# Other half-steps for the side work of six batches, ScalarE in pieces of 512 columns, wider block turns

## The chip, the cores and the metric

The kernel runs on one core of a Trainium2 chip. The metric is device time in microseconds of one execution; the kernel before has a median of 707.55 us in three runs. Times below are microseconds unless marked ns. PE is TensorE's matmul queue, PEld its weight loads, DVE VectorE, ACT ScalarE, POOL GpSimd, SP the engine that issues most DMAs (SPq in the rows).

## What is computed

An attention through 32 memories per head, followed by a two-layer network with a squared ReLU. Cut to what matters:

```python
a = softmax(phi, over the sequence)               # B 8, H 8, S 576, M 32
k_m, v_m = a^T k, a^T v                           # per head 32 x 64
attn = softmax(q k_m^T / 8, over the memories)    # S x 32 per head
x = (attn v_m) laid out as tokens x 512           # 4608 x 512
h = max(x w_in, 0)                                # w_in 512 x 2048
out = (h * h) w_out                               # w_out 2048 x 512
```

The kernel never forms x. Per batch it folds v_m into w_in, which gives `u` (four chunks n = 0 to 3 of 512 columns of w_in, as a high and a low part), and the first layer multiplies `u` with the attention weights `a` (also high and low). Both are split so that three fast products stand for one exact product.

## The kernel before, in words

**Two parts ahead of the second layer.** Batches 0 and 1 run through `runs`, a list of steps that interleaves both layers (up to about 213 us). Batches 2 to 7 run in the loop at the end of the function: per batch 16 steps (f = 0 to 15, 128 rows of the hidden layer each), and then one second layer for all six (from 427 us). This document is about the loop.

**A step** of the loop: `first_layer(b, f, ...)` puts 12 matmuls of 128x288 (two halves of the tokens) into a PSUM tile `hh`, of which there are two; ScalarE then takes ReLU of it into half of a tile `o` (`r`); `half(2 * k)` and `half(2 * k + 1)` write out the side work that is due in the two half-steps; `spill()` writes a full `o` (two steps, 576 KB) to the DRAM tensor `r_f`. There are two `o` tiles, so the third pair of steps waits until the first one's spill has landed, and the matmuls of step f+2 wait for the ReLU of step f.

**Side work** of batch b is the table `later`: for each task the half-steps (of 32 per batch, counted from the batch's first) in which its parts are issued, and the batch it is for, as an offset.

- `task_phi`, `task_kv`, `task_q`: loads, all on SP's queue, which issues in order.
- `task_exp` (`exp_phi_blocks`): the maximum of phi over the sequence on DVE (`phi_mx`, `top`), the subtraction into `e_sb`, then Exp on ACT. It is for the batch after the next.
- `task_mem` (`memories_in_h`): 80 small matmuls of `e_sb` with the loaded k and v, normalised into a tile `st` and turned in 32x32 blocks into `mem`.
- `task_u` (`make_u`): 16 matmuls into the one tile `ps_m`, a copy to `u_hi` on ACT, the rest to `u_lo` on DVE, which frees `ps_m`.
- `task_attend` (`attend`): 8 pairs of score matmuls from `q_sb` (one buffer), then on DVE block turns into `st`, maximum, subtraction, on ACT Exp, on DVE sum, reciprocal, product, block turns into `at`; on ACT the high part `a_hi` (or `o`, `r_room`, which also serve as rooms for it), on POOL the low part.

Engines take their instructions in the order in which the loop writes them, so the table fixes each engine's queue. In it the k-th step of a batch is written out before the side work of half-steps 2k and 2k+1. `STEP` is 32 half-steps, `begin` the first of batch 2 (`FUSED`). A task whose list passes 32 runs into the next batch: `task_u, 1, 2` at 32 to 34 is chunk 2 of the batch that has just begun.

Of the kernel before, what the change touches and what calls it, by code (L numbers as in the profile page):

```python
# [8 lines left out]
F32 = mybir.dt.float32  # L9
# [3 lines left out]
AF = mybir.ActivationFunctionType  # L13
ALU = mybir.AluOpType
# [10 lines left out]
def attn_moe_kernel(ctx: ExitStack, tc: tile.TileContext, qT, kv, phi, w_in, w_out, outT):  # L25
# [20 lines left out]
    D = 64  # L46
    M = 32
# [182 lines left out]
    def exp_phi_blocks(b, e):  # L230

        w = NQ * P
        nb = w // M
        mx = one.tile([P, w], F32, name="phi_mx")
        nc.vector.tensor_tensor(out=mx, in0=e[0], in1=e[1], op=ALU.max)
        for x in e[2:-1]:
            nc.vector.tensor_tensor(out=mx, in0=mx, in1=x, op=ALU.max)  # L237
# [4 lines left out]
        tr = one.tile([P, w], F32, name="at")  # L242
# [12 lines left out]
        for x in e[:-1]:  # L255
            nc.vector.tensor_tensor(out=x, in0=x, in1=mx, op=ALU.subtract)
# [40 lines left out]
    def memories_in_h(b, kvs, mem):  # L297


        assert ("phi", b) in ready  # L300
# [16 lines left out]
        ready.add(("read", b))  # L317
        den = work.tile([P, NQ], F32, name="den")
        kvn = one.tile([P, 2, NQ, 2, D], F32, name="st")
        for qd in range(NQ):  # L320
            nc.vector.tensor_scalar_add(den[:, qd:qd + 1], acc[qd][:, 2 * D:2 * D + 1], EPS)
            nc.vector.reciprocal(den[:, qd:qd + 1], den[:, qd:qd + 1])
            nc.vector.tensor_scalar_mul(
                kvn[:, :, qd],
                acc[qd][:, :2 * D].rearrange("p (x d) -> p x d", x=2)[:, :, None, :].broadcast_to([P, 2, 2, D]),
                den[:, qd:qd + 1],
            )
        yield
# [233 lines left out]
    def make_u(b, n, mem, w, got):  # L562
# [9 lines left out]
        nc.scalar.copy(u_hi[:, :, n0:n1], ps[:, :, :n1 - n0])  # L572
# [407 lines left out]
    for n in kept:  # L980
# [63 lines left out]
        ((87, 88, 88), task_mem, 2),  # L1044
# [17 lines left out]
        ((112, 113, 113), task_u, 2, 2),  # L1062
# [11 lines left out]
    for places, fn, *args in plan:  # L1074
# [9 lines left out]
        ((2, 3, 5), task_mem, 1),  # L1084
        ((3,), task_phi, 2),
        ((4, 6, 8, 10, 12), task_kv, 2, 0),
        ((14, 16, 18, 20, 22), task_kv, 2, 1),
        ((8, 9, 10), task_u, 0, 3),
        ((9, 10, 11, 12, 13, 14, 15), task_attend, 1, 0),
        ((10,), task_q, 1, 1),  # L1090
        ((16, 17, 18), task_u, 1, 0),
        ((18, 19, 20, 21, 22, 23, 24), task_attend, 1, 1),
        ((19,), task_q, 2, 0),
        ((24, 25, 26), task_u, 1, 1),
# [410 lines left out]
```

## Time and profile before

| | |
|---|---|
| median of three runs | 707.55 us (706.66 to 708.33) |
| the profiled execution: its own time, its span | 708.06 us, 706.2 us |
| PE busy | 686.6 us, 97% of the span |
| DVE, ACT, POOL busy | 531.6, 395.8, 59.1 us |
| granted TensorE clock | 0.999 |
| from batch 3's memories (221.48 us) to batch 7's (369.04 us) | four periods of one batch each |
| second layer begins | 427.12 us |

The granted clock is at its upper level (2.4 GHz) throughout. In the rows, a timeline line reads: start, duration, engine, source line, operation, output<-inputs, shape, count, and in brackets the idle time of the engine before it and what ended it. Matmuls of one step stand in six lines of two; the line with `a_hi,u_hi` begins a step.

### The profile page before, as it was taken

The numbers are of one execution on the slowest core, as the hardware profiler recorded it, in microseconds if no ns is written. First come the engines' busy times: TensorE is split into PE (matmuls) and PEld (weight loads), VectorE is DVE, ScalarE is ACT, GpSimd is POOL, SyncE is SP. The second block draws the span as 40 slices with busy tenths as digits, with TensorE's granted clock in tenths as the row PEclk, the third lists the DMA queues.
The fourth block names the chain that finished last, engine by engine and source line by source line (L and its number), as shares of the span: only waits on it lengthen the run. The fifth ranks groups of instructions, "written<-read, shape, count | busy, mean of one in ns | idle before, by whom it ended". The sixth has DMA issues, their size and how long they took to land.

```text
span 706.2 us, 14494 instructions
## 1 busy us (share of the span) xinstructions
PE 686.6 (97%) x5860; PEld 612.8 (87%) x5860; DVE 531.6 (75%) x967; ACT 395.8 (56%) x575; POOL 59.1 (8%) x86
## 2 busy tenths in 40 slices
PE   9899999999999989899989999999999999999997
PEld 4477798988888778787878899999999999999996
DVE  4978797987776686867676403989988979697984
ACT  2648887866553444444444546766655565555551
POOL 1222102102220000000000000000000000000000
PEclk9999999999999999999999999999999999999999
DMA  9992537354794949494954358753364544435331
GB/s 307 391 349 104 199 111 230 103 168 131 203 342 152 322 162 315 158 319 165 316 188 168 146 201 301 262 174 111 90 180 119 151 120 129 140 117 153 90 120 60
DMA packets 94354, 133.58 MB, mean 189 GB/s; under 512 B 5520, under 2 KB 59408, under 8 KB 93648
## 3 DMA queue, kind: packets, MB, share of 16 engines
q1 hardware_dynamic: 91472, 127.62, 56.2%
q10 hardware_dynamic: 2816, 5.05, 1.9%
q8 instruction: 46, 0.75, 0.4%
q14 instruction: 20, 0.16, 0.1%
HBM read 86.51 MB, written 46.14 MB: 188 GB/s over the span
## 4 chain that ended last, share of the span: by engine, by line
PE 76%; DVE 12%; DMA 4%; ACT 4%; issue 2%; SPq 0%; POOL 0%; ACTq 0%; DVEq 0%
PE b L1293 33%; PE hh L1425 11%; PE acc L743 10%; PE h L692 7%; PE b L1276 5%; PE acc L735 3%; PE ps_m L426 3%; PE h L304 2%; DMA r_f<-o 2%; DMA wo<-in_w_in 1%; DVE phi_mx L237 1%; DMA u_hi<-in_kv 1%; DVE at L488 1%; DVE st L485 1%; DVE sm L474 1%
## 5 line engine op out<-in xcount | busy, mean ns | idle before, releaser
L1227 DVE TENSOR_TENSOR x_lo<-y,x_hi 128x1792 fp32r<-128x1792 f32 (+1 forms) x56 | 104.7, 1870 | 49.7 <-ACT x_hi L1223 49.7
L1223 ACT CAST x_hi<-y 128x1792 fp32r<-128x1792 f32 (+1 forms) x56 | 87.9, 1570 | 96.2 <-PE b L1293 52.1
L1293 PE MATMUL b<-x_lo,s_hi 128*128 128x256 f32 x384 | 108.1, 281 | 0.0
L1293 PE MATMUL b<-x_hi,wo 128*128 128x256 f32 x576 | 107.9, 283 | 0.0
L1293 PE MATMUL b<-x_hi,s_hi 128*128 128x256 f32 x384 | 107.9, 281 | 0.0
L1293 PE MATMUL b<-x_hi,s_lo 128*128 128x256 f32 x384 | 107.9, 281 | 0.0
L1456 ACT ACTIVATE o<-hh 128x576 f32<-128x576 f32 x94 | 60.8, 650 | 68.2 <-PE hh L1425 37.7
L1293 PEld LDWEIGHTS b<-x_hi,wo 128*128 128x128 f32 x576 | 89.9, 192 | 0.0
L1293 PE MATMUL b<-x_lo,wo 128*128 128x256 f32 x288 | 81.5, 283 | 0.4 <-DVE x_lo L1227 0.3
L574 DVE TENSOR_TENSOR u_lo<-ps_m,u_hi 128x1024 fp32r<-128x1024 f32 (+1 forms) x33 | 39.3, 1190 | 52.6 <-ACT u_hi L572 52.4
L1216 DVE TENSOR_TENSOR y<-y 128x512 f32<-128x512 f32 x144 | 73.7, 512 | 3.4
L1293 PEld LDWEIGHTS b<-x_hi,s_hi 128*128 128x128 f32 x384 | 73.7, 192 | 0.0
L1293 PEld LDWEIGHTS b<-x_lo,s_hi 128*128 128x128 f32 x384 | 72.1, 188 | 0.0
L1293 PEld LDWEIGHTS b<-x_hi,s_lo 128*128 128x128 f32 x384 | 72.1, 188 | 0.0
L1206 ACT ACTIVATE y<-raw 128x1024 f32<-128x1024 f32 (+1 forms) x56 | 57.4, 1025 | 12.3 <-DMA raw<-r_f 9.8
L1293 PEld LDWEIGHTS b<-x_lo,wo 128*128 128x128 f32 x288 | 55.3, 192 | 0.8 <-DVE x_lo L1227 0.8
L1425 PEld LDWEIGHTS hh<-a_hi,u_hi 128*128 128x128 f32 x188 | 29.3, 188 | 24.8 <-ACT o L1456 14.9
L1425 PE MATMUL hh<-a_hi,u_hi 128*128 128x288 f32 x188 | 44.4, 317 | 3.4 <-ACT o L1456 3.2
L743 PE MATMUL acc<-g_hi,wo 128*128 128x320 f32 (+1 forms) x256 | 43.2, 301 | 0.0
L1425 PE MATMUL hh<-a_hi,u_lo 128*128 128x288 f32 x188 | 40.2, 295 | 0.0
L1425 PE MATMUL hh<-a_lo,u_hi 128*128 128x288 f32 x188 | 40.1, 294 | 0.0
L700 ACT ACTIVATE r_room<-h 128x320 f32<-128x320 f32 (+2 forms) x56 | 24.7, 441 | 27.5 <-PE h L692 26.6
(234 smaller groups left out, 1442.2 us busy)
## 6 DMA issues: line engine op xcount, KB each, us to landing
r_f<-o SPq DMA_DIRECT2D x48, 576.0 KB, 4.4
raw<-r_f SPq DMA_DIRECT2D x48, 512.0 KB, 4.0
wo<-in_w_in SPq DMA_DIRECT2D x16, 512.0 KB, 8.2
wo<-in_w_out SPq DMA_DIRECT2D x16, 512.0 KB, 6.9
kvb<-in_kv SPq DMA_DIRECT2D x28, 256.0 KB, 6.2
q_sb<-in_q SPq DMA_DIRECT2D x24, 288.0 KB, 5.1
out_t<-m SPq DMA_DIRECT2D x24, 256.0 KB, 2.3
e_sb<-in_phi SPq DMA_DIRECT2D x8, 512.0 KB, 4.3
```

Of the source, the lines that this page charges most:

```text
L574: nc.vector.tensor_tensor(out=u_lo[:, :, n0:n1], in0=ps[:, :, :n1 - n0], in1=u_hi[:, :, n0:n1].bitcast(F32), op=ALU.subtract)
L692: nc.tensor.matmul(h[:, at:at + n], u[:, qd, fs], x[:, qd], start=(i == 0), stop=(i == len(todo) - 1))
L700: nc.scalar.activation(r, h[:, :T], AF.Relu)
L743: nc.tensor.matmul(acc[e][:, :T], wo[f][:, w, e * P:(e + 1) * P], x, start=first and x is g_hi and w == 0, stop=last and x is g_lo,)
L1206: nc.scalar.activation(y[i][:, :2 * n], raw.pop(i), AF.Square)
L1216: nc.vector.tensor_tensor(out=out, in0=in0, in1=in1, op=ALU.subtract)
L1223: nc.scalar.copy(x[i][0], y[i])
L1227: nc.vector.tensor_tensor(out=x[i][1], in0=y.pop(i), in1=x[i][0].bitcast(F32), op=ALU.subtract)
L1276: nc.tensor.matmul(acc[e][:, :n], wo[f][:, v, e * P:(e + 1) * P], x[i][u][:, f % 2 * n:(f % 2 + 1) * n], start=f == 0 and j == 0, stop=f = ...
L1293: nc.tensor.matmul(acc[m][:, e * HALF:(e + 1) * HALF], w, x[i][u][:, z * HALF:(z + 1) * HALF], start=p == 0 and e == 0 and j == 0, stop=p ...
L1425: nc.tensor.matmul(banks[t][:, :T], u[:, qd, fs], x[:, qd], start=(i == 0), stop=(i == len(todo) - 1))
L1456: nc.scalar.activation(r.rearrange("p (t x) -> p t x", t=NT), h[:, :, :S // NT], AF.Relu)
```

## The change

It rewrites the table `later` (every task at other half-steps; Exp of phi ends at half-step 26 instead of 31; chunk 2 of `u` is now listed under its own batch, at 0, 1, 3; memories begin at 1 instead of 2; the load of the second half of q goes from 10 to 12, the scores that read it from 18 to 17). For batch 2 alone memories stay later, at 4 to 8, and phi and the k and v loads shift by 3. ScalarE's copy to `u_hi` becomes two of 512 columns, Exp of `e_sb` two of 512 and one of 128. In `memories_in_h` the product with 1/den goes from DVE to ACT (`kvn`, without the second copy that it had), and 8 block turns of 32x(4x32) replace 16 of 32x(2x32). In `exp_phi_blocks` the maximum becomes a tree with a second tile, and four subtractions become one of 1024 columns. From batch 4 on, that second tile is `a_hi1` instead of `at`.

```diff
+        tr = place([P, w], F32, name="a_hi1") if b > FUSED + 1 else one.tile([P, w], F32, name="at")
         nc.vector.tensor_tensor(out=mx, in0=e[0], in1=e[1], op=ALU.max)
-        for x in e[2:-1]:
-            nc.vector.tensor_tensor(out=mx, in0=mx, in1=x, op=ALU.max)
+        nc.vector.tensor_tensor(out=tr, in0=e[2], in1=e[3], op=ALU.max)
+        nc.vector.tensor_tensor(out=mx, in0=mx, in1=tr, op=ALU.max)
...
-        for x in e[:-1]:
-            nc.vector.tensor_tensor(out=x, in0=x, in1=mx, op=ALU.subtract)
+        nc.vector.tensor_tensor(
+            out=full, in0=full, in1=mx[:, None, :].broadcast_to([P, nfull, w]), op=ALU.subtract
+        )
...
-        nc.scalar.activation(e_sb[:, :nfull], e_sb[:, :nfull], AF.Exp)
-        nc.scalar.activation(e[nfull], e[nfull], AF.Exp)
+        for x in (full[:, :2], full[:, 2:], e[nfull]):
+            nc.scalar.activation(x, x, AF.Exp)
...
+        yield
         den = work.tile([P, NQ], F32, name="den")
-        kvn = one.tile([P, 2, NQ, 2, D], F32, name="st")
         for qd in range(NQ):
             nc.vector.tensor_scalar_add(den[:, qd:qd + 1], acc[qd][:, 2 * D:2 * D + 1], EPS)
-            nc.vector.reciprocal(den[:, qd:qd + 1], den[:, qd:qd + 1])
-            nc.vector.tensor_scalar_mul(
...
+        nc.vector.reciprocal(den, den)
+        yield
+        kvn = one.tile([P, 2, NQ, D], F32, name="st")
+        for qd in range(NQ):
+            nc.scalar.activation(
+                kvn[:, :, qd], acc[qd][:, :2 * D].rearrange("p (x d) -> p x d", x=2), AF.Copy,
+                scale=den[:, qd:qd + 1],
             )
...
-                    nc.vector.transpose(
-                        mem[at:at + M, x, j // 2::2], kvn[M * j:M * (j + 1), x, :, 0, M * k:M * (k + 1)]
-                    )
+                nc.vector.transpose(
+                    mem[at:at + M, :, j // 2::2], kvn[M * j:M * (j + 1), :, :, M * k:M * (k + 1)]
+                )
...
-        nc.scalar.copy(u_hi[:, :, n0:n1], ps[:, :, :n1 - n0])
+        for half in range(2) if b >= FUSED else (slice(2),):
+            nc.scalar.copy(u_hi[:, half, n0:n1], ps[:, half, :n1 - n0])
...
     later = [
-        ((2, 3, 5), task_mem, 1),
...
-        ((24, 26, 27, 28, 29, 31), task_exp, 2),
...
+        ((1, 2, 5, 6, 7), task_mem, 1),
...
+        ((12, 13, 16, 17, 21, 26), task_exp, 2),
...
```

**ScalarE, second half of batch 5** (`o` ReLU of a step, L471 and L474 Exp of the scores, L491 and L494 the high part of the weights, L261 to L264 Exp of `e_sb`). Before:

```order
L1456 ACTIVATE o_4314<-hh 128x576
L1456 ACTIVATE o_4381<-hh 128x576
L471 ACTIVATE st<-st 128x576
L1456 ACTIVATE o_4381<-hh 128x576
L1456 ACTIVATE o_4426<-hh 128x576
L491 CAST o_4410<-at 128x576
L572 CAST u_hi_4430<-ps_m 128x1024
L1456 ACTIVATE o_4426<-hh 128x576
L1456 ACTIVATE o_4487<-hh 128x576 x2
L261 ACTIVATE e_sb<-e_sb 128x1024
L262 ACTIVATE e_sb<-e_sb 128x128
L1456 ACTIVATE o_4527<-hh 128x576
```

After:

```order
L1463 ACTIVATE o_4365<-hh 128x576 x2
L474 ACTIVATE st<-st 128x576
L576 CAST u_hi_4386<-ps_m 128x512 x2
L1463 ACTIVATE o_4422<-hh 128x576 x2
L264 ACTIVATE e_sb<-e_sb 128x512 x2
L264 ACTIVATE e_sb<-e_sb 128x128
L494 CAST o_4404<-at 128x576
L1463 ACTIVATE o_4458<-hh 128x576 x2
L1463 ACTIVATE o_4488<-hh 128x576
```

Exp of `e_sb` stood behind the last ReLU of the batch and ahead of the first of the next; now it stands two steps earlier, behind step 13, with the high part of the weights right behind it.

**VectorE, the same stretch** (`phi_mx`, `top`: the maximum of phi; L574 and L578 `u_lo`; L457 to L488, L460 to L491 the softmax of the scores). Before:

```order
L240 TENSOR_TENSOR phi_mx<-phi_mx,e_sb 64x128 x2
L574 TENSOR_TENSOR u_lo_4431<-ps_m,u_hi_4430 128x1024
L243 STREAM_TRANSPOSE at<-phi_mx 128x256
L245 TENSOR_REDUCE top<-at 128x8
L248 TENSOR_TENSOR top<-top 32x8 x3
L250 COPY top<-top 32x8 x3
L252 COPY at<-top 128x256
L253 STREAM_TRANSPOSE phi_mx<-at 128x256
L256 TENSOR_TENSOR e_sb<-e_sb,phi_mx 128x256 x4
L258 TENSOR_TENSOR e_sb<-e_sb,phi_mx 64x128 x2
L574 TENSOR_TENSOR u_lo_4530<-ps_m,u_hi_4529 128x1024
```

After:

```order
L255 STREAM_TRANSPOSE phi_mx<-a_hi_4233 128x256
L578 TENSOR_TENSOR u_lo_4261<-ps_m,u_hi_4260 128x1024
L460 STREAM_TRANSPOSE st<-h 128x288 x2
L466 TENSOR_REDUCE mx<-st 128x18
L472 TENSOR_TENSOR st<-st,mx 128x576
L257 TENSOR_TENSOR e_sb<-e_sb,phi_mx 128x1024
L261 TENSOR_TENSOR e_sb<-e_sb,phi_mx 64x128 x2
L477 TENSOR_REDUCE sm<-st 128x18
L480 TENSOR_SCALAR sm<-sm 128x18
L483 RECIPROCAL sm<-sm 128x18
L488 TENSOR_TENSOR st<-st,sm 128x576
L491 STREAM_TRANSPOSE at<-st 128x576
```

The maximum of phi stood behind the second softmax of the batch; now it stands around the first, and the subtraction into `e_sb` in the middle of the second.

**SP, first half of batch 5** (`r_f` spills, `kvb` and `tmp` loads of k and v). Before:

```order
L1412 DMA r_f_0_96<-o_4059 256x1x576
L294 DMA kvb_109<-in_kv 128x4x128
L294 DMA kvb_110<-in_kv 128x4x128
L1412 DMA r_f_1_97<-o_4164 256x1x576
L294 DMA kvb_111<-in_kv 128x4x128
L415 DMA q_sb<-in_q 128x2x288 x2
L294 DMA kvb_112<-in_kv 128x4x128
L1412 DMA r_f_2_98<-o_4204 256x1x576
```

After:

```order
L296 DMA kvb_109<-in_kv 128x4x128
L1419 DMA r_f_0_96<-o_4027 256x1x576
L296 DMA kvb_110<-in_kv 128x4x128
L296 DMA kvb_111<-in_kv 128x4x128
L1419 DMA r_f_1_97<-o_4122 256x1x576
L296 DMA kvb_112<-in_kv 128x4x128
L296 DMA kvb_113<-in_kv 64x4x128
L1419 DMA r_f_2_98<-o_4178 256x1x576
L418 DMA q_sb<-in_q 128x2x288 x2
```

The load of q stood ahead of the third spill, now it stands behind it.

## Rows read from the trace of the kernel before

**Rows 1.** Windows: length, PE, PEld, DVE, ACT, POOL busy, clock, DMA share, GB/s.

```profile
221.48:258.49 37.01, 34.72 (x369) 28.83 (x368) 26.07 (x66) 15.03 (x23) 3.05 (x6) 1.00 0.81 258
...
332.20:369.04 36.84, 34.84 (x369) 28.81 (x369) 26.61 (x65) 17.26 (x27) 3.07 (x6) 1.00 0.77 242
369.04:400.83 31.79, 31.62 (x340) 26.99 (x341) 19.23 (x44) 16.37 (x25) 2.85 (x2) 1.00 0.42 150
```

**Rows 2.** Timeline of PE, end of batch 5, two lines before which it idled.

```profile
359.39 0.54 PE L1425 MATMUL hh<-a_hi,u_hi 128*128 128x288 f32 x2 [0.37 <-ACT o L1456]
...
369.04 1.09 PE L304 MATMUL h<-kvb,e_sb 128*32 128x130 f32 x32 [1.24 <-ACT e_sb L261]
```

**Rows 3.** Timeline of PE, batch 6 and start of batch 7.

```profile
385.40 0.53 PE L1425 MATMUL hh<-a_hi,u_hi 128*128 128x288 f32 x2
387.20 0.72 PE L426 MATMUL h<-q_sb,mem 64*32 64x288 f32 x16
...
397.46 0.53 PE L1425 MATMUL hh<-a_hi,u_hi 128*128 128x288 f32 x2 [0.17 <-ACT o L1456]
...
400.83 1.09 PE L426 MATMUL ps_m<-w,mem 64*32 64x512 f32 x16
...
403.54 0.42 PE L1425 MATMUL hh<-a_hi,u_hi 128*128 128x288 f32 x2
405.13 0.42 PE L1425 MATMUL hh<-a_hi,u_hi 128*128 128x288 f32 x2
```

**Rows 4.** Timeline of DVE, second half of batch 5.

```profile
353.20 0.84 DVE L457 STREAM_TRANSPOSE st<-h 128x288 f32<-128x288 f32 x2
...
356.37 0.75 DVE L474 TENSOR_REDUCE sm<-st 128x18 f32<-128x576 f32 x1 [0.75 <-ACT st L471]
...
358.53 0.78 DVE L488 STREAM_TRANSPOSE at<-st 128x576 f32<-128x576 f32 x1
...
359.65 2.15 DVE L237 TENSOR_TENSOR phi_mx<-phi_mx,e_sb 128x256 f32<-128x256 f32 x2
...
362.47 1.23 DVE L574 TENSOR_TENSOR u_lo<-ps_m,u_hi 128x1024 fp32r<-128x1024 f32 x1
...
364.53 0.54 DVE L248 TENSOR_TENSOR top<-top 32x8 f32<-32x8 f32 x3
...
366.46 1.43 DVE L256 TENSOR_TENSOR e_sb<-e_sb,phi_mx 128x256 f32<-128x256 f32 x4
```

**Rows 5.** Timeline of POOL, second half of batch 5.

```profile
360.10 1.42 POOL L492 TENSOR_TENSOR o<-at,o 128x576 fp32r<-128x576 f32 x1 [7.91 <-ACT o L491]
```

**Rows 6.** Timelines of POOL and DVE, batch 6, an overlap of the two.

```profile
396.02 1.43 POOL L492 TENSOR_TENSOR g_room<-at,r_room 128x576 fp32r<-128x576 f32 x1 [8.02 <-ACT r_room L491]
...
396.89 1.23 DVE L574 TENSOR_TENSOR u_lo<-ps_m,u_hi 128x1024 fp32r<-128x1024 f32 x1 [1.66 <-ACT u_hi L572]
```

**Rows 7.** Timeline of ACT, second half of batch 5.

```profile
355.65 0.69 ACT L471 ACTIVATE st<-st 128x576 f32<-128x576 f32 x1 [1.88 <-DVE st L469]
...
359.92 1.01 ACT L572 CAST u_hi<-ps_m 128x1024 fp32r<-128x1024 f32 x1
...
363.42 0.66 ACT L1456 ACTIVATE o<-hh 128x576 f32<-128x576 f32 x1 [1.32 <-PE hh L1425]
367.93 1.06 ACT L261 ACTIVATE e_sb<-e_sb 128x1024 f32<-128x1024 f32 x1 [3.85 <-DVE e_sb L256]
```

**Rows 8.** Timeline of SP, batch 5: the load of q's second half.

```profile
341.18 1.00 SPq L415 DMA_DIRECT2D q_sb<-in_q  x2
```

**Rows 9.** The loads of `q_sb`, batches 2 to 5 (221 to 369 us).

```profile
DMA to landing us min/median/max: 3.4/5.3/6.4
```

**Rows 10.** The loads of `q_sb`, batch 6 (370 to 427 us).

```profile
DMA to landing us min/median/max: 3.1/3.6/4.1
```

**Rows 11.** Timeline, batch 2's memories: DVE's block turns, PE's scores.

```profile
176.26 2.99 DVE L335 STREAM_TRANSPOSE mem<-st 32x64 f32<-32x64 f32 x16
...
177.80 2.07 PE L426 MATMUL ps_m<-q_sb,mem 64*32 64x288 f32 x16
```

More of the change, by code (lines that the diff above doesn't have):

```diff
@@ L233, in exp_phi_blocks @@
         nb = w // M
+        nfull = S // P
+        full = e_sb[:, :nfull]
         mx = one.tile([P, w], F32, name="phi_mx")
+        tr = place([P, w], F32, name="a_hi1") if b > FUSED + 1 else one.tile([P, w], F32, name="at")
         nc.vector.tensor_tensor(out=mx, in0=e[0], in1=e[1], op=ALU.max)
-        for x in e[2:-1]:
-            nc.vector.tensor_tensor(out=mx, in0=mx, in1=x, op=ALU.max)
+        nc.vector.tensor_tensor(out=tr, in0=e[2], in1=e[3], op=ALU.max)
+        nc.vector.tensor_tensor(out=mx, in0=mx, in1=tr, op=ALU.max)
         at = [(slice(D * qd, D * (qd + 1)), slice(P * qd, P * (qd + 1))) for qd in range(NQ)]
@@ L241, in exp_phi_blocks @@
         yield
-        tr = one.tile([P, w], F32, name="at")
         nc.vector.transpose(tr, mx)
@@ L259, in exp_phi_blocks @@
         yield
-        nfull = S // P
-        nc.scalar.activation(e_sb[:, :nfull], e_sb[:, :nfull], AF.Exp)
-        nc.scalar.activation(e[nfull], e[nfull], AF.Exp)
+        for x in (full[:, :2], full[:, 2:], e[nfull]):
+            nc.scalar.activation(x, x, AF.Exp)
         ready.add(("phi", b))
@@ L297, in memories_in_h @@
     def memories_in_h(b, kvs, mem):
-        assert ("phi", b) in ready
+        assert ("phi", b) in ready and all(len(x) == NCH for x in kvs.values())
         acc = [ps_h.tile([P, 512], F32, name="h") for _ in range(NQ)]
@@ L332, in memories_in_h @@
             for k in range(2):
-                for x in range(2):
-                    at = M * (2 * (j % 2) + k)
-                    nc.vector.transpose(
-                        mem[at:at + M, x, j // 2::2], kvn[M * j:M * (j + 1), x, :, 0, M * k:M * (k + 1)]
-                    )
+                at = M * (2 * (j % 2) + k)
+                nc.vector.transpose(
+                    mem[at:at + M, :, j // 2::2], kvn[M * j:M * (j + 1), :, :, M * k:M * (k + 1)]
+                )
         ready.add(("mem", b))
@@ L1043, in attn_moe_kernel @@
         ((78, 80, 80, 82, 82), decode_out, 15, nc.gpsimd),
-        ((87, 88, 88), task_mem, 2),
+        ((87, 87, 87, 88, 88), task_mem, 2),
         ((87, 90), ahead, 0),
@@ L1061, in attn_moe_kernel @@
         ((107, 108, 109), task_u, 2, 1),
-        ((112, 113, 113), task_u, 2, 2),
         ((2,), lambda: spin(3, ident)),
@@ L1083, in attn_moe_kernel @@
     later = [
-        ((2, 3, 5), task_mem, 1),
[L1085 to L1094, printed above, removed]
-        ((24, 26, 27, 28, 29, 31), task_exp, 2),
-        ((32, 33, 34), task_u, 1, 2),
+        ((0, 1, 3), task_u, 0, 2),
+        ((1, 2, 5, 6, 7), task_mem, 1),
+        ((2,), task_phi, 2),
+        ((3, 5, 7, 9, 11), task_kv, 2, 0),
+        ((13, 15, 17, 19, 21), task_kv, 2, 1),
+        ((6, 7, 9), task_u, 0, 3),
+        ((9, 10, 11, 14, 15, 15, 19), task_attend, 1, 0),
+        ((12,), task_q, 1, 1),
+        ((17, 18, 19, 22, 23, 23, 27), task_attend, 1, 1),
+        ((14, 15, 17), task_u, 1, 0),
+        ((18,), task_q, 2, 0),
+        ((12, 13, 16, 17, 21, 26), task_exp, 2),
+        ((22, 23, 25), task_u, 1, 1),
     ]
@@ L1100, in attn_moe_kernel @@
             if b + x < B:
+                if b == FUSED and fn is task_mem:
+                    places = (4, 4, 5, 6, 8)
+                elif b == FUSED and fn in (task_phi, task_kv):
+                    places = [p + 3 for p in places]
                 at([begin + STEP * (b - FUSED) + p for p in places], fn, b + x, *args)
```

3 lines of the change are left out of this document (removed).

## Prediction

> **What bounds the kernel now.** I read the windows first, one for each stretch from one batch's memory matmuls to the next batch's. The four periods from 221.48 to 369.04 take 147.56 us together; the first is 37.01, the last 36.84 [rows 1]. PE is busy for 34.84 of the 36.84 us, DVE for 26.61, ACT for 17.26, and the clock is granted in full: PE bounds the loop, and the other engines have room on average. So the question is where PE waits, which the timeline of PE shows. In batch 5 it idles 1.24 us ahead of the memory matmuls, waiting for ACT's Exp of `e_sb`, and 0.37 us ahead of a step whose PSUM tile ACT has not yet emptied [rows 2]. Idle time undercounts, since the ends of matmuls are modelled, so I price the waits by starts. Batch 6 has no phi to prepare and hardly waits. From its memory matmuls to chunk 2 of batch 7 it takes 31.79 us [rows 1]; that task and the step behind it take 400.83 to 403.54, 2.71 us [rows 3]. Together 34.50, with one wait of 0.17 in it [rows 3], so a period with no wait costs 34.33. Four of them are 137.3 us: 10.2 of the 147.56 us are waits, and with batch 6's 0.17 there are 10.4 us that an order of side work could win in the loop. The matmuls are the same in number and shape in both kernels, so that is a ceiling.
>
> Where the waits come from: ACT stands idle 3.85 us ahead of Exp of `e_sb`, waiting for DVE's subtraction [rows 7], and the next batch's first ReLU is queued behind. DVE gets there late because the maximum of phi is queued behind the second softmax. And one part of it is slow: two maxima take 2.15 us [rows 4], the second of them beginning just when POOL's low part runs, 360.10 for 1.42 us [rows 5].
>
> **The change, part by part.** *Exp of e_sb.* It moves to two steps before the batch's end. If it is done by then, its four waits go: 1.24 idle each, some 5.0 us in all. What is late next has to be worked out along ACT's and DVE's new queues. I count from the end of step 7 of a batch, with a step at 1.60 us (403.54 to 405.13), one between two side tasks at 1.80 (385.40 to 387.20), the scores at 0.72 at most, and a chunk of `u` with its step at 2.71 [rows 3]. PE then ends step 8 at 2.8, the scores at 3.5, step 11 at 8.5, step 12 at 11.2, step 13 at 12.8, step 14 at 14.4, step 15 at 16.1. ACT does ReLU (0.66) and Exp of the first scores (0.69) [rows 7] by 1.5. DVE follows with sum to block turn, 356.37 to 359.31, 2.94 us, by 4.45; the rest of phi's maximum, 364.53 to 366.46, 1.93 us, by 6.4; `u_lo`, 1.23, by 7.6 [rows 4]; and block turns to subtraction of the second scores, 353.20 [rows 4] to 355.65 [rows 7], 2.45 us, by 10.05. ACT, free since step 11's ReLU, waits for that by some 1 us, then has Exp until 10.75 and two half copies to `u_hi`: one of 1024 columns takes 1.01 [rows 7], two of 512 perhaps 1.1, until 11.85, and ReLU of step 12 until 12.5. PE needs it at 12.8: 0.3 us to spare. DVE subtracts into `e_sb` (1.43 for the four that become one [rows 4], and two short ones, say 1.9 together) by 11.95 and ends the second softmax at 14.9. ACT has ReLU 13 until 13.5, Exp of `e_sb` in three pieces (1.06 for the large part [rows 7], some 1.4 with the small one and the split) until 14.9, the high part of the weights, about 0.65, until 15.55, and ReLU 14 until 16.2, for which PE waits from 16.1 on. So in place of a batch's 2.5 us of waits I put 0.1 to 0.15 here. Exp is done at 14.9, the memory matmuls come at about 18.7: 3.8 us to spare.
>
> *POOL's low part.* The first one now follows the cast behind step 9, at about 5.9 to 7.3, while DVE does the end of phi's maximum and `u_lo`; the second meets hardly any DVE work. In batch 6 such a `u_lo` ran beside POOL (396.02 to 397.45) and took 1.23 as ever [rows 6]. By these rows the collision of 1.3 us is gone. The Trainium skill (GPSIMD Engine Reference, specifications) says that GpSimd shares SBUF's interfaces with VectorE's instructions that use two ports or have two SBUF inputs, and `u_lo` reads PSUM: by that rule too nothing is lost, unless POOL meets the subtraction into `e_sb`, which would then cost up to 1.4; the rows put the two 2.7 us apart.
>
> *Block turns and the product on ACT.* 16 turns take 2.99 us [rows 11], 8 of twice the width between 1.5 and 3.0. In the loop DVE has this time to spare and ACT's two small copies lie behind step 2, with a PE step of 1.60 to cover them, so I cost both at nothing; without cover, 0.3 a copy. In batch 2 it counts: its scores take 2.07 [rows 11] where 0.72 is the usual [rows 3], 1.35 of it waiting for the turns. But ACT's two copies now stand ahead of a copy that DVE's split waits for, and that split stands ahead of the turns. I take a gain of 0.3, between a loss of 0.8 and a gain of 1.35.
>
> *The load of q for the second attention.* This is the one transfer that comes closer to its use. It moves behind the third spill, and its reader moves forward by a step. Counting from the end of step 5: ReLU until 0.86, the spill's issue some 0.5 (two issues take 1.00 [rows 8]), so the second half of q goes out at about 1.9; PE reads it after steps 6 and 7, a chunk of `u` and step 8, at 1.60 + 1.69 + 2.82 = 6.1. It has 4.2 us. Loads of q landed in 3.4 to 6.4, median 5.3, beside those of k, v and phi [rows 9], and in 3.1 to 4.1 without [rows 10]. Which applies depends on the queue ahead of it. Before, q goes out at 341.18 [rows 8], 9.0 us after the memory matmuls began at 332.20 [rows 1]; the loads wait for these matmuls' end, some 2 us, so phi, three pieces of k and v and two spills, 2.5 MB by their shapes, are issued in about 7 us. Now memory matmuls, steps 1 to 3 (5.0), a chunk with step 4 (2.8), scores (0.7), step 5 (1.7) and ReLU and spill (1.4) make 14 us, less the same 2, for 3.5 MB. That is a lower rate, 0.29 in place of 0.36 MB a us, so the queue should be nearly empty by then, but for the spill just issued. I take 4.4 us, a wait of 0.2, and keep 0 and 2.2 as bounds.
>
> The Trainium skill (DMA: Bandwidth & Descriptors, Anatomy of one DMA) has about 2.0 us plus bytes over 436 GB/s for a transfer alone, an estimate of 2.7 us for this one; by it q is never late and 0.8 us less would be lost. The rows without load, 3.1 to 4.1, are longer, and they decide.
>
> **The sum.** 10.4 us of waits, less 4 x 0.35 that stay (ACT's end 0.15, q 0.2), less 0.1 in batch 6, plus 0.3 in batch 2: 9.2 us. The profiled execution took 708.06 (span 706.2); 698.9 by it. The median of the runs is 0.5 below it, 707.55, so 698.3.
>
> **Rivals.** *DVE a little later.* The 0.3 us ahead of step 14 is all there is. If DVE is 1.3 later (POOL stops `u_lo` or the subtraction after all), step 14 waits 1.0 and ReLU 14 another 0.3: 1.3 a period, 5 us in all, 703.5. For it: that much did happen at the maxima [rows 4, 5]. Against it: [rows 6].
>
> *q late.* At the median [rows 9] it lands 1.1 after PE asks, at their maximum 2.2: 0.9 to 2.0 more a period than I put, 701.9 to 706.3. For it: every load of q under load but the quickest took longer than 4.2. Against it: the rate above.
>
> *Slower: the queue falls behind.* The same place, past a point. Each period has 2.3 us of net gain to lose, so from a landing 6.7 us after the issue on (q's rows reach 6.4) the kernel is slower, by 0.4 us for each 0.1; at 7.2 us it is 709.5. For it: a shorter period asks the same bytes in less time, with DMA busy for 0.77 of it before [rows 1]. Against it: spills and loads of k and v come no closer together ahead of q.
>
> **How the numbers follow.** Forecast 0.58 (696.2 to 700.5), DVE later 0.14, q late 0.18, slower 0.07, and 0.03 for waits that come back elsewhere and leave about the time of before. A measurement of this kernel tells 0.2%, 1.4 us. Faster by more: 0.88; within: 0.05 (the 0.03, and the seam of q late and slower); slower: 0.07. The range begins where all waits are gone and batch 2 gains 1.0 (707.55 - 10.4 - 1.0 = 696.2) and reaches through DVE later to 703.6, leaving out the upper part of q late (0.08), slower and the rest, 0.18.
>
> **What would show it.** Right: the periods are 34.4 to 34.9 us; no wait of PE for ACT's `e_sb` is left; DVE's maxima of phi are all near 0.4; ACT waits about 1 us ahead of the second Exp of scores. Wrong: PE waits ahead of the scores, with `q_sb` landing last (q late); PE waits at step 14 with ACT's Exp of scores waiting for DVE by over 2 us (DVE later); periods above 36.9 (slower). If the periods shrink and the total does not, the second layer's start has taken it back, which I have given next to nothing.

## The result, and the profile after

The changed kernel takes 701.19 us (median of four runs, 700.51 to 702.42), beside 707.88 for the kernel before in the same set (706.66 to 708.33): a ratio of 0.9916, 95% interval 0.9902 to 0.9929. It is faster, by 6.7 us where 9.2 were forecast. The profiled execution took 700.55 us, its span 698.8, against 708.06 and 706.2 before.

First the periods, as in [rows 1]. The windows of the changed kernel, from one batch's memory matmuls to the next batch's (length, PE, PEld, DVE, ACT, POOL busy, clock, DMA share, GB/s). The first is no full period, since memory matmuls now stand two steps earlier in a batch from batch 3 on; the last ends at batch 7's memory matmuls:

```profile
222.35:253.93 31.58, 31.58 (x346) 25.63 (x345) 22.32 (x51) 16.93 (x30) 3.16 (x6) 1.00 0.85 278
253.93:288.75 34.82, 34.81 (x376) 28.75 (x369) 23.31 (x51) 18.55 (x33) 3.22 (x6) 1.00 0.78 254
288.75:324.61 35.86, 35.24 (x377) 28.86 (x369) 23.69 (x51) 18.43 (x33) 3.21 (x6) 1.00 0.77 249
324.61:359.32 34.71, 34.71 (x376) 28.78 (x368) 23.31 (x51) 18.55 (x33) 3.21 (x6) 1.00 0.78 258
```

36.84 to 37.01 became 34.71 and 34.82, but the one of batch 4 is 35.86. The timeline of PE at the end of batch 5 (start, duration, line) answers to [rows 2]: the memory matmuls now follow chunk 2 of `u` with no idle time, and nothing waits for `e_sb`:

```profile
358.31 1.09 PE L429 MATMUL ps_m<-w,mem 64*32 64x512 f32 x16
359.32 1.09 PE L306 MATMUL h<-kvb,e_sb 128*32 128x130 f32 x32
```

Why that is so stands on DVE and ACT. DVE's timeline in batch 5, maximum of phi, `u_lo`, second softmax and `e_sb`, against [rows 4]:

```profile
338.15 0.42 DVE L239 TENSOR_TENSOR a_hi<-e_sb 128x256 f32<-128x256 f32 x1
338.61 0.42 DVE L240 TENSOR_TENSOR phi_mx<-phi_mx,a_hi 128x256 f32<-128x256 f32 x1
...
346.44 1.19 DVE L578 TENSOR_TENSOR u_lo<-ps_m,u_hi 128x1024 fp32r<-128x1024 f32 x1
...
349.87 1.22 DVE L257 TENSOR_TENSOR e_sb<-e_sb,phi_mx 128x1024 f32<-128x1024 f32 x1
...
353.78 0.78 DVE L491 STREAM_TRANSPOSE at<-st 128x576 f32<-128x576 f32 x1
```

and ACT's (idle time before it and its releaser in brackets), against [rows 7]:

```profile
349.99 0.69 ACT L474 ACTIVATE st<-st 128x576 f32<-128x576 f32 x1 [0.27 <-DVE st L472]
350.58 1.06 ACT L576 CAST u_hi<-ps_m 128x512 fp32r<-128x512 f32 x2
352.16 0.65 ACT L1463 ACTIVATE o<-hh 128x576 f32<-128x576 f32 x1 [0.52 <-DMA r_f<-o]
...
354.01 1.34 ACT L264 ACTIVATE e_sb<-e_sb 128x512 f32<-128x512 f32 x3
355.25 0.66 ACT L494 CAST o<-at 128x576 fp32r<-128x576 f32 x1
355.81 0.65 ACT L1463 ACTIVATE o<-hh 128x576 f32<-128x576 f32 x1
```

The maxima that took 2.15 us for two take 0.42 each. Exp of `e_sb` ends at 355.35, 4.0 us before PE wants it, where it ended with PE waiting. The 1.06 us for two half copies to `u_hi` against 1.01 for the whole one [rows 7], and 1.34 us for three pieces of Exp, are the price of the pieces.

Batch 4 is told by PE's timeline ahead of its second scores:

```profile
307.94 1.40 PE L429 MATMUL h<-q_sb,mem 64*32 64x288 f32 x16 [0.60 <-DVE st L488]
```

The bracket names DVE's `st` of line 488, which ended at 307.88. But in batch 5 the scores begin at 343.08 while that instruction runs (342.95 to 343.71), so they do not wait for it; what came last was the load of q, 0.13 us ahead. Its row for the two issues ahead of these scores, in batch 4 and then in batch 5 (against [rows 9, 10]):

```profile
DMA to landing us min/median/max: 5.1/5.2/5.3
```

```profile
DMA to landing us min/median/max: 4.0/4.1/4.2
```

In batch 4 the halves of q land at 307.8 and 308.6, 5.1 and 5.9 after the first was issued (302.73), and PE asked at 307.3, 4.5 us after that issue. By starts, the step and the scores there cost 1.35 us over what they cost in a batch that does not wait; in batches 2, 3, 5 and 6 the scores cost 0.24, 0.25, 0.25 and 0.08 over.

**Where the 7.4 us between the two spans lie**, by the starts of the same PE instructions:

| stretch | before | after | difference |
|---|---|---|---|
| up to batch 2's memory matmuls (same instructions) | 171.28 | 170.98 | -0.30 |
| these matmuls to the step behind batch 2's scores | 8.53 | 8.65 | +0.12 |
| from there to the loop's first steps | 33.65 | 33.10 | -0.55 |
| to the second layer | 213.66 | 206.29 | -7.37 |
| the second layer | 279.08 | 279.78 | +0.70 |

### The profile page after: what moved, and what is told of

Same layout as the page of the kernel before. It is cut to its first block, busy times and chain, and to the rows that moved or that the text cites. A ratio compares the mean times of both kernels' runs of the same rounds, so it can differ in the third digit from the quotient of the medians.

```text
span 698.8 us, 14434 instructions
## 1 busy us (share of the span) xinstructions
PE 686.7 (98%) x5860; PEld 613.1 (88%) x5860; DVE 515.2 (74%) x883; ACT 402.8 (58%) x617; POOL 59.7 (9%) x86
## 4 chain that ended last, share of the span: by engine, by line
PE 89%; DMA 5%; DVE 3%; ACT 1%; issue 0%; ACTq 0%; POOL 0%; DVEq 0%
PE b L1300 33%; PE hh L1432 22%; PE acc L747 11%; PE h L696 7%; PE ps_m L429 5%; PE b L1283 4%; PE acc L739 3%; PE h L306 2%; DMA wo<-in_w_out 1%; DMA wo<-in_w_in 1%; PE h L429 1%; DMA wo<-in_kv 1%; DMA kvb<-in_kv 1%; DVE x_lo L1234 1%; PE h L1432 0%
## 5 line engine op out<-in xcount | busy, mean ns | idle before, releaser
L578 DVE TENSOR_TENSOR u_lo<-ps_m,u_hi 128x1024 fp32r<-128x1024 f32 (+1 forms) x33 | 38.8, 1176 | 13.3 <-ACT u_hi L576 13.1
```

Of the source, the lines that this page charges most:

```text
L578: nc.vector.tensor_tensor(out=u_lo[:, :, n0:n1], in0=ps[:, :, :n1 - n0], in1=u_hi[:, :, n0:n1].bitcast(F32), op=ALU.subtract)
```

## Experiments

Each kernel differs from the changed one or from the one before by the diff shown; ratios are against the kernel before in the same set of runs, whose medians were 709.03, 707.98 and 707.16 us.

**The load of q put back.** If q is the term that was too small, its issue alone gives the difference back.

```diff
-        ((12,), task_q, 1, 1),
+        ((10,), task_q, 1, 1),
```

> The changed kernel, with only the load of the second half of q put back from half-step 12 to 10, ahead of the third spill. Theory (the load of q is the term that was sized too small: scores held up by 0.24, 0.25, 1.35, 0.25 and 0.08 us in batches 2 to 6 of the changed kernel's profile, 2.2 us in all): these go, and the time is 698.8 to 699.5 against 701.2. Rival 1 (batch 4's 1.35 us is DVE's block turns holding the PSUM tile, as the trace names it): 1.0 to 1.4 us stay, 700.3 to 701. Rival 2 (the queue is late as a whole, so the third spill is now late and a ReLU waits for its tile): no gain, 701 to 702.

Measured: 699.21 us (698.81 to 699.64), ratio 0.9860 (0.9847 to 0.9874). The changed kernel was not run in this set, in which the kernel before was about 1 us slower than in the others. Its windows of PE (length, busy, clock, DMA share, GB/s):

```profile
254.06:288.53 34.47, 34.47 (x377) 1.00 0.80 259
288.53:323.03 34.50, 34.50 (x376) 1.00 0.79 258
```

Batch 4 is like the others, no wait over 0.2 us is left in the loop, and neither the third spill nor DVE took its place: both rivals fall. A period with no idle time costs 34.47 us in this table, not the 34.33 that I had from the kernel before.

**The load of q a step later still.**

```diff
-        ((12,), task_q, 1, 1),
+        ((14,), task_q, 1, 1),
```

> The changed kernel with the load of the second half of q at half-step 14 instead of 12, one step later. Theory (from here on every microsecond by which q goes out later is one that PE waits): 1.6 us or somewhat more in each of five batches, 708 to 711, so the whole gain is gone. Rival (landing is set by what else is queued, not by the issue): 701 to 704.

Measured: 706.93 us (705.60 to 709.44), 0.9988 (0.9975 to 1.0002): the gain is gone, though not quite as far as was expected. PE in batch 2, both halves of the scores waiting:

```profile
239.56 0.69 PE L429 MATMUL h<-q_sb,mem 64*32 64x288 f32 x8 [1.37 <-DVE at L491]
240.43 0.69 PE L429 MATMUL h<-q_sb,mem 64*32 64x288 f32 x8 [0.18 <-DMA q_sb<-in_q]
```

In batches 2 to 5 PE is held up by 2.3, 1.3, 1.9 and 1.5 us where the changed kernel lost 0.24, 0.25, 1.35 and 0.25. Counted from the memory matmuls, q's first half goes out only 0.65 to 0.7 us later in batches 2 to 4 (1.3 in batch 5), but there a load of k and v now stands between it and the third spill, and its halves go out 1.0 us apart instead of 0.6: in batch 2 it lands 1.9 us later, in batch 3 0.9, and PE waits 2.1 and 1.1 longer. What counts one to one is the landing, not the issue.

**The changed kernel again.** No edit.

> The changed kernel once more, beside the kernels of this set. Expected: 700.5 to 702.5, with the scores of one batch in five held up by over 1 us by q (batch 4 in the first profile) and the others by 0.1 to 0.3. If the hold-up belongs to batch 4's place in the queue it is batch 4 again; if it is chance, another batch or none.

Measured: 702.27 us (701.50 to 703.85), 0.9925 (0.9904 to 0.9946). The periods of batches 3 to 5 are 35.02, 36.14 and 34.71 us, and PE's row ahead of batch 4's scores is nearly the same:

```profile
308.94 1.40 PE L429 MATMUL h<-q_sb,mem 64*32 64x288 f32 x16 [0.56 <-DVE st L488]
```

So it is batch 4 again, and not chance. Its place in the queue is that of every batch. What differs shows in the section of DMA queues for the 2 us in which q's first half moves (queue and kind, packets, MB, share of 16 engines; kernel as changed, 305.73 to 307.81 us):

```profile
q14 instruction: 1, 0.01, 0.9%
```

There is one packet on a queue of the kind "instruction" beside q's; in the second profile one lies at 307.0 to 307.5. Counting each engine's instructions up to such packets, many of these come when VectorE or ScalarE has done 63 or so more than a multiple of 128 (VectorE 575 in this case), so this one should be VectorE's code.

**VectorE's code moved, not its work.**

```diff
     make_identity(nc, ident)
+    spare = const.tile([P, 8], F32, name="spare")
+    for _ in range(30):
+        nc.vector.memset(spare, 0.0)
```

> The changed kernel with 30 small memsets on VectorE at the very start, where it waits for its first load (they cost nothing there). They change only when VectorE fetches its next block of instructions. Theory (batch 4's long wait for q is such a fetch: in both profiles of the changed kernel one small instruction packet runs at 306 to 307 us, while q is under way, and q's transfer takes 2.05 us beyond the queue where 0.8 to 1.3 is usual): the packet that now comes at 306 comes near 283 us, and the scores of batch 4 are held up by 0.2 to 0.5 us instead of 1.35 to 1.5; the time is about 1 us less, 0.990 to 0.9915 of the kernel before. Rival (it belongs to batch 4's place in the queue): 1.3 to 1.5 us there as before, and the ratio stays at 0.992.

Measured: 701.30 us (701.11 to 701.48), 0.9912 (0.9899 to 0.9926). The packet is now at 284 us, and none lies in the window in which batch 4's q moves; the load lands sooner, and PE has no idle time ahead of the scores (rows: the packet at 283.5 to 284.5; q's two issues in batch 4; PE):

```profile
q14 instruction: 1, 0.01, 2.0%
```

```profile
DMA to landing us min/median/max: 3.9/4.1/4.3
```

```profile
307.47 1.11 PE L432 MATMUL h<-q_sb,mem 64*32 64x288 f32 x16
```

By starts these scores cost 0.39 over, not 1.35: in batch 4 the theory holds. Whether the time followed can't be told: the ratio lies in the theory's range and within noise of the rival's 0.992, and the span is 699.4 us beside the changed kernel's 698.8 and 700.2. In this profile q held PE up longer in the other batches, by 0.50, 0.64, in batch 5 by 1.0 and in batch 6 by 0.46, 3.0 us in all for the 2.2 of the changed kernel's first; and batch 5's q took 4.7 us to land with no such packet near it. So the packet is the likely reason why it was batch 4 (one profile without it), and not the reason for the size of the term.

**The table alone, the operations alone.** Both halves of the change apart.

```diff
-        for x in (full[:, :2], full[:, 2:], e[nfull]):
-            nc.scalar.activation(x, x, AF.Exp)
+        nc.scalar.activation(full, full, AF.Exp)
+        nc.scalar.activation(e[nfull], e[nfull], AF.Exp)
...
-        for half in range(2) if b >= FUSED else (slice(2),):
+        for half in (slice(2),):
```

and in the same way the chain of maxima, the four subtractions, the product on DVE and 16 block turns.

> The changed kernel's table with all operations as before: one Exp of 1024 columns, product on DVE with 16 block turns, four subtractions, a chain of maxima, one copy to u_hi. Theory (the table carries the gain, the operations cost nothing in the loop and 0.3 us in batch 2): 701 to 702. Rival (the operations carry a part, because without them DVE is late at the end of a batch, where 0.3 us were to spare): a wait of 0.3 to 1.0 us at step 14 in four batches, 702.5 to 705.5.

Measured: 701.19 us (699.78 to 701.71), 0.9884 (0.9867 to 0.9901), as fast as the changed kernel or a little faster. Its periods of batches 3 to 5 are 35.16, 34.87 and 34.69: the new table does it all. In batch 3 a step waits 0.5 us, in batch 4 q costs 0.43; its VectorE has other counts of instructions, and no instruction packet meets q there.

The other way round, the kernel before with the operations changed and its own table (the chain of maxima kept, the parts of the memories at the old half-steps):

```diff
-        nc.scalar.activation(e_sb[:, :nfull], e_sb[:, :nfull], AF.Exp)
-        nc.scalar.activation(e[nfull], e[nfull], AF.Exp)
+        for x in (full[:, :2], full[:, 2:], e[nfull]):
+            nc.scalar.activation(x, x, AF.Exp)
...
-        ((2, 3, 5), task_mem, 1),
+        ((2, 2, 2, 3, 5), task_mem, 1),
```

> The kernel before, its table kept, with the operations changed alone: Exp in three pieces, product on ACT with 8 block turns, one subtraction of 1024 columns, copies to u_hi in halves; the maxima stay a chain. Theory (operations are worth nothing in the loop as long as Exp of e_sb comes at the batch's end): 707 to 708, and in batch 2 the scores lose 0.4 us or so while the memory matmuls gain 0.35. Rival (half pieces and fewer DVE operations shorten the chain to the memory matmuls by 0.3 to 0.5 us in four batches): 705.5 to 706.7.

Measured: 707.61 us (705.62 to 708.40), 0.9977 (0.9964 to 0.9989). The four periods sum to 146.76 us, 0.8 less than [rows 1]: the wait for Exp of `e_sb` is shorter, but it stays. The median and the span (706.0 us for 706.2) are the theory's; by the ratio it is 1.6 us, the rival's figure, so a gain of up to 0.2% stays open in the old table. None of it adds to the new one, where the chain has room.

**One task moved alone.** The kernel before, with only the preparation of `e_sb` at its new half-steps (and its scratch tile in `a_hi1` from batch 4 on, as in the change).

```diff
-        ((24, 26, 27, 28, 29, 31), task_exp, 2),
+        ((12, 13, 16, 17, 21, 26), task_exp, 2),
```

> The kernel before with one task moved: the maximum of phi, the subtraction and Exp of e_sb at half-steps 12, 13, 16, 17, 21, 26 instead of 24 to 31 (the scratch tile goes with it). Theory (the waits for Exp of e_sb are about 5.0 us, the collision of the maxima with POOL another part of the 10.4): 700.5 to 703, no wait of PE for e_sb left. Rival (before's second softmax and this work get in each other's way on DVE, and the waits come back at the steps behind the second scores): 704 to 707.5.

Measured: 723.71 us (722.84 to 725.48), 1.0209 (1.0192 to 1.0226): far slower, and outside both expectations. Its waits, over the loop (what waited, for what: total, times, longest), ACT in batch 4, PE's next step, and the windows of PE of the wait and behind it:

```profile
PE hh L1425 <- ACT o L1456: 17.8, 13, 2.3
```

```profile
333.84 0.67 ACT L491 CAST r_room<-at 128x576 fp32r<-128x576 f32 x1 [2.95 <-DVE at L488]
334.42 1.01 ACT L572 CAST u_hi<-ps_m 128x1024 fp32r<-128x1024 f32 x1
335.32 0.66 ACT L1456 ACTIVATE o<-hh 128x576 f32<-128x576 f32 x1
```

```profile
336.03 0.53 PE L1425 MATMUL hh<-a_hi,u_hi 128*128 128x288 f32 x2 [2.28 <-ACT o L1456]
```

```profile
331.99:336.03 4.04, 1.76 (x14) 1.00 0.26 97
336.03:340.94 4.91, 4.91 (x25) 0.65 0.47 177
```

No wait for `e_sb` is left, as expected. But DVE now comes late to the second softmax, ACT's high part of the weights waits for it, and the ReLU that empties PE's tile is queued behind that. Part of the loss is the clock: behind that wait it was granted at 0.65, and the next two steps take 2.09 and 2.82 us where steps in such places take 1.69, 1.5 us more. That comes in each of four batches, some 6 of the 14.7 us by which the four periods are longer than in [rows 1]. The changed table moves that high part from 24 to 27, behind the ReLU of step 13, and the first softmax's from 15 to 19. Without the rest of the table, moving `e_sb` is a loss of 2%.

**VectorE later by 1.5 us**, with q at 10, to price the rival "DVE a little later". The copy and block turn of the maximum of phi are done three times in four batches:

```diff
-        nc.vector.tensor_copy(tr.rearrange("p (k x) -> p k x", k=nb), ...)
-        nc.vector.transpose(mx, tr)
+        for _ in range(3 if b > FUSED + 1 else 1):
+            nc.vector.tensor_copy(tr.rearrange("p (k x) -> p k x", k=nb), ...)
+            nc.vector.transpose(mx, tr)
```

> The changed kernel with q back at 10, and with VectorE's copy and block turn that spread the maximum of phi done three times instead of once in four batches: 1.5 us of VectorE's time more, ahead of the second softmax's subtraction. Theory (0.3 us is all there is to spare ahead of step 14): 1.2 to 1.5 us a batch, 704 to 705.2 against the 699.2 with q alone, the wait at step 13 or 14 behind ScalarE's ReLU. Rival (ScalarE's wait for VectorE in that place is slack that takes it in): under 0.4 us a batch, below 701.

Measured: 707.23 us (705.84 to 708.33), 0.9991 (0.9979 to 1.0003): 8.0 us or 2.0 a batch over the kernel with q at 10 (2.1 by the periods), more than was added. DVE, POOL and PE in batch 3:

```profile
278.16 0.29 DVE L255 COPY a_hi<-top 128x256 f32<-128x256 f32 x1
...
278.97 1.11 DVE L255 COPY a_hi<-top 128x256 f32<-128x256 f32 x1
...
280.49 1.18 DVE L579 TENSOR_TENSOR u_lo<-ps_m,u_hi 128x1024 fp32r<-128x1024 f32 x1
```

```profile
278.50 1.42 POOL L496 TENSOR_TENSOR a_lo<-at,a_hi 128x576 fp32r<-128x576 f32 x1 [20.29 <-ACT a_hi L495]
```

```profile
281.72 0.63 PE L430 MATMUL ps_m<-u_hi,mem 64*32 64x512 f32 x4 [1.35 <-DVE u_lo L579]
```

The third copy met POOL's low part and took 1.11 for 0.29, so DVE was later by 2.3 us and not by 1.5. And the first to wait was not step 14 but chunk 1 of `u` at step 11, whose PSUM tile DVE's `u_lo` frees. With q at 10 alone, `u_lo` ends at 277.08 and chunk 1 starts at 278.15: 1.1 us are to spare there, and 2.3 less 1.1 is about the 1.35 of the row. The steps at the batch's end cost 0.6 more. So DVE has little to give in both places.

**Two joints of PE closed.** With q at 10, periods had no idle time and still cost more than 34.33. By starts, a step that stands next to a side task takes 1.69 us, one between two side tasks 1.79, one among steps 1.60 (the single steps of [rows 3]). Before, chunk 3 of `u` and the first scores stood in a row and took 0.88 and 0.62; apart they take 1.02 and 0.65. The kernel before, timeline of PE, end of the chunk and the scores right behind it:

```profile
266.24 0.61 PE L426 MATMUL ps_m<-u_lo,mem 64*32 64x512 f32 x4
266.64 0.69 PE L426 MATMUL h<-q_sb,mem 64*32 64x288 f32 x16
```

The changed one, the same chunk in batch 5, with a step ahead of the scores:

```profile
332.36 0.61 PE L429 MATMUL ps_m<-u_lo,mem 64*32 64x512 f32 x4
...
334.67 0.71 PE L429 MATMUL h<-q_sb,mem 64*32 64x288 f32 x16
```

The experiment closes this joint, and makes a second one of chunk 0 and the second scores.

```diff
-        ((6, 7, 9), task_u, 0, 3),
+        ((9, 9, 11), task_u, 0, 3),
...
-        ((12,), task_q, 1, 1),
+        ((10,), task_q, 1, 1),
+        ((17, 17, 18), task_u, 1, 0),
         ((17, 18, 19, 22, 23, 23, 27), task_attend, 1, 1),
-        ((14, 15, 17), task_u, 1, 0),
```

> The changed kernel with q back at 10, and two chunks of u written out right beside the scores (chunk 3 at 9, 9, 11; chunk 0 at 17, 17, 18 ahead of the scores). Theory (a side task between two steps costs PE 0.19 us in its two neighbours, and two tasks side by side share that; before, chunk 3 and the first scores stood so and the change parted them): each joint gives back about 0.2 us, 0.4 a period, 1.6 to 2.2 us in all, 697.0 to 697.7 against the 699.2 with q alone. Rival (the copies to u_hi and the rest u_lo now fall between the scores and their softmax, which then ends later): no gain, waits of 0.3 us or more at steps 13 and 14, 699 to 701.

Measured: 694.61 us (694.52 to 696.16), 0.9819 (0.9799 to 0.9840), which beats both kernels. Of it, chunk 3 alone (`task_u, 1, 0` left at 14, 15, 17):

> The changed kernel with q back at 10 and one of the two joints closed: chunk 3 of u right ahead of the first scores (9, 9, 11), chunk 0 left at 14, 15, 17. Theory (each joint is worth the same, 0.34 us a period each): periods of 34.1 to 34.2, 697.3 to 697.8. Rival (the gain of the two together sits in the other joint, the one ahead of the scores that q held up): 34.4 and 699.

Measured: 697.02 us (695.62 to 698.30), 0.9852 (0.9834 to 0.9869). Windows of PE in batch 4, first with one joint closed, then with both:

```profile
287.74:321.90 34.16, 34.16 (x376) 1.00 0.80 261
```

```profile
286.89:320.69 33.80, 33.80 (x376) 1.00 0.80 263
```

34.50, 34.16, 33.80: each joint is worth 0.34 to 0.36 us a period, more than the 0.2 that I first expected, and both are alike. I had counted the step between the two tasks alone (1.79 against 1.60); the tasks themselves also take 0.17 less in a row (0.88 and 0.62 against 1.02 and 0.65). The ratios, from three sets, are too coarse to part the two. The copies and `u_lo` that now fall between the scores and their softmax make nothing wait: that rival falls.

**Batch 2's scores**, on top of that kernel: the row block's low part (`split_out`, line 679) written out behind the block turns.

```diff
-        ((87, 87), split_out, 1),
+        ((87, 89), split_out, 1),
```

> The kernel with q at 10 and the two joints closed, in which one VectorE operation of batch 2's stretch (the low part of a row block of w_out, line 679, 0.7 us, which waits for ScalarE's two copies) is written out behind the 8 block turns instead of ahead of them. Theory (the turns themselves are not late, they stand behind that operation): batch 2's scores go from 1.4 us of wait to 0.2 or less, 693.0 to 693.6 against 694.6. Rival (matmuls a step later need that row block, and wait for it instead): a gain under 0.4 us.

Measured: 694.51 us (694.28 to 694.79), 0.9818 (0.9804 to 0.9831): no gain, the rival's figure, though the cause was right and no matmul waits for the row block. In the changed kernel DVE does

```profile
175.77 0.69 DVE L679 TENSOR_TENSOR wo<-tmp,wo 128x512 fp32r<-128x512 f32 x1 [1.91 <-ACT wo L676]
176.38 2.56 DVE L338 STREAM_TRANSPOSE mem<-st 32x128 f32<-32x128 f32 x8
```

and PE's scores take 2.46 us beside that. Here the turns go from 174.50 to 177.07 and the scores take 0.71. But further on the next chunk of `u` meets a load that lands when it did before (weight loads of PE, its idle time and releaser):

```profile
205.28 0.15 PEld L429 LDWEIGHTS ps_m<-u_lo,mem 64*32 64x32 f32 x8 [0.68 <-DMA u_lo<-w_f]
```

That costs 0.8 by starts (the kernel before lost 0.57 at the same load). In the loop, steps of batches 4 and 5 wait for ACT's ReLU, which takes 0.9 from the two periods. PE got ahead, and other things were not ready; why those ReLUs came late was not followed up.

## Why the prediction was right, and where it was off

The gain came where it was forecast, from the waits for Exp of `e_sb` and from what stood behind them; by the spans 7.4 of the 9.2 us came.

**Waits for Exp of `e_sb` and the chain behind it: right.** All four went. I had counted, from the end of step 7, DVE ready with the second scores at 10.05 us, ACT free for step 12 at 12.5, Exp of `e_sb` at 14.9, ReLU of step 14 at 16.2. Counted from chunk 0 in batch 5 (340.29) these ends are 9.7, 12.5, 15.1 and 16.2. ACT's wait ahead of the second Exp was 0.27, not 1, since DVE was 0.4 earlier and PE a little later, and ReLU of step 12 waits for its `o` tile's spill to land, which I had not counted; the end came out the same. By starts PE loses 0.17 us there in batches 4 and 5 and 0.27 in batch 3 (five steps take 8.33, 8.33 and 8.43, and 8.16 in batch 6, which has no Exp of `e_sb`), where I put 0.10 to 0.15. The 3.8 us to spare for the memory matmuls are 4.0.

**POOL's collision: right, with a condition.** The maxima take 0.42. `u_lo` beside POOL takes 1.19 (346.44 to 347.63, POOL from 347.16 on), as [rows 6] had said, and a copy from SBUF beside POOL took nearly four times its time in the experiment with DVE later. The rule of the Trainium skill (GPSIMD Engine Reference, specifications) that the prediction cited agrees for `u_lo`; the copy has one input in SBUF, and would fall under it only by using two ports, which no row shows.

**Block turns and the product on ACT: nothing in the loop is right, the gain in batch 2 was not.** The table alone gives the same periods. In batch 2 I took a gain of 0.3; it is a loss of 0.12. The memory matmuls gained 0.35 and the scores lost 0.46 (2.46 for 2.00), since the 8 turns take 2.56 us, not 1.5, and wait for the split that waits for ACT: the mechanism that I named for the loss, inside its bound, but weighed too low.

**The load of q: the median right, the tail missed.** This is the step that failed: "I take 4.4 us, a wait of 0.2". Four batches of five have 0.24, 0.25, 0.25 and 0.08; batch 4 has 1.35. Together these are 2.2 us, where the sum has 0.9, and each is within the bound of 2.2 a period. The first half landed 4.0 us after its issue and in batch 4 5.1, the second 0.8 later than the first. PE asks 4.5 us after the first issue, so what counts is when the second half lands (4.8), and one value was too little for a wait that can grow but not fall below nothing. With q back at 10 the time is less by 2.0 and 3.1 us by medians against the changed kernel's two, 1.9 and 3.3 by the profiles' spans, 0.0056 and 0.0065 of the time by the ratios (4.0 and 4.6 us); from batch 3's memory matmuls to the second layer it is 2.3 and 3.0. The estimate of 2.7 us from the Trainium skill (DMA: Bandwidth & Descriptors, Anatomy of one DMA) went by a fit that the page gives for DMAs on GpSimd's path, while this load is issued by SP; the halves took 3.9 to 5.3.

**The floor: the right number, by luck.** I took the matmuls as the same and so a period without waits as the same, 34.33. With q at 10 a period takes 34.47 and shows no idle time, but a wait is left in it. In that kernel ACT's ReLU and PE at the end of batch 3, and PE at the end of batch 6, which has no Exp of `e_sb`:

```profile
285.01 0.65 ACT L1463 ACTIVATE o<-hh 128x576 f32<-128x576 f32 x1
285.71 0.53 PE L1432 MATMUL hh<-a_hi,u_hi 128*128 128x288 f32 x2
287.51 1.09 PE L429 MATMUL ps_m<-w,mem 64*32 64x512 f32 x16
```

```profile
389.13 0.42 PE L1432 MATMUL hh<-a_hi,u_hi 128*128 128x288 f32 x2
390.81 1.09 PE L429 MATMUL ps_m<-w,mem 64*32 64x512 f32 x16
```

Batch 3's step begins at 285.71, right behind the ReLU that ends at 285.66, and takes 1.80 us for the 1.68 of batch 6; five steps take 8.34 there for 8.16. This 0.17 is the wait at the batch's end that the prediction had put at 0.10 to 0.15, and the floor is 34.30. With it the changed kernel's periods add up: floor, batch's end and q make 34.82, 35.82 and 34.72, measured 34.82, 35.86 and 34.71.

So 34.33 fits the new table, but it was not the floor of the old one. For batch 6's wait the prediction took off the idle 0.17, though it meant to price waits by starts. The step ahead of it:

```profile
395.54 0.43 PE L1425 MATMUL hh<-a_hi,u_hi 128*128 128x288 f32 x2
```

It takes 1.92 us, up to 397.46, and the next one 1.70 [rows 3], where 1.60 is the usual: 0.4. And the step behind chunk 2 has no memory matmuls behind it there, 0.1 more. The old floor is thus about 34.2, and the new order costs 0.1 a period: it parts chunk 3 and the first scores, 0.36 by the joints experiment, and puts chunk 2 right ahead of the memory matmuls, which gives part of it back (that was not tried apart). The joints experiment shows that there was more to win than waits: with both closed the loop takes 3.4 us less (from batch 3's memory matmuls to the second layer 190.99 us for 194.37), and the ceiling of 10.4 that I drew was none.

**The second layer took 0.7 us back**, in part the case that the prediction's last sentence named. Part of it is a wait of 0.47 us for DVE's `x_lo` at 449 us. It hangs on a `raw` load that took 6.4 us (5.3 before). But the kernel with the old table and new operations, whose second layer begins at 426.18, needs 279.8 us for it too, and over thirteen profiles of these kernels it is 279.1 (the kernel before) to 280.3, with no clear order by the time at which it begins. I take it for scatter of the transfers; it was not tried apart.

**The sum.** 1.3 for q, 0.2 at the batch's end, 0.4 for batch 2 and 0.7 for the second layer are short of the forecast. Two things outside its terms came on top, by luck: 0.55 behind batch 2 (a load of `u_lo` that landed in time here) and 0.3 ahead of it. That makes 700.6 by this account, for 700.55 measured. The rival "DVE a little later" did not happen, but the experiment makes it dearer than I had it: 2.0 a batch for 1.5 added, with chunk 1 of `u` the first to wait. "The queue falls behind" did not happen either; one step further it does, and the gain is gone.

## What to carry to other kernels

When a table of side work is rewritten, count the borders between long and short work on the bounding engine, besides waits: they cost the same in every period, show up as no idle time, and here two of them were worth about as much as the late transfer (3.4 us of the loop for 2.3 to 3.0). Set a load's issue by the latest landing that the queue has shown for its last piece, since a load that was early cost nothing here while its buffer was free, and one that was late cost as much as it was late. And move a chain as a whole: the one task that held the end of the batch up, moved alone, put its work ahead of something more urgent and cost 2%, some two fifths of it through the granted clock.

## What the runs showed of the hardware

- A small instruction packet beside a transfer went with a long one in batch 4 of the changed kernel: q's first half took 5.1 us to land with it (two profiles), 3.9 with the packet elsewhere (one). It is no rule: loads of q took 4.0 with such a packet (q at 10, batch 2), and 4.7 and 5.2 without one (the moved code, batch 5; q at 14, batch 2). The packet itself held 0.9% of 16 engines for 2.08 us, 0.3 us of one; how this makes 1.1 is not shown. The page of the changed kernel has 46 and 21 such packets (queue and kind, packets, MB, share of 16 engines):

```profile
q8 instruction: 46, 0.75, 0.5%
q14 instruction: 21, 0.17, 0.1%
```

  These are 16 KB and 8 KB each. The Trainium skill (Runtime: NRT & Kernel Launch, Instruction fetch mechanics) has it that an engine refills its instructions in blocks of 16 KiB through its own DMA queue, and that crossing a block is mostly hidden. The 16 KiB agree with the first row and not with the second; whether a load beside it pays nothing, the rows here leave open.
- In the kernel with one task moved, the granted clock of the 4.9 us behind a wait of PE of 2.28 us was 0.65 on average, part at the lower level of 1.2 GHz and part at the upper of 2.4, and 1.00 behind that. In the kernel with DVE later, where PE waited 1.35 us a batch, it stayed at 1.00, the upper level.
- The border between a step and a side task on PE: 1.69 us for a step with one such neighbour, 1.79 with two, 1.60 with none, with PE shown as busy throughout. Two side tasks in a row take 0.88 and 0.62 us, apart 1.02 and 0.65.
